# Mirrored output pairs for an inverse DFT: eight matmuls and a flip for two tiles, in place of sixteen matmuls

## The chip, the cores and the metric

The kernel runs on one core of one Trainium2 chip. The metric is the device time of a whole run in microseconds (us). The kernel before takes about 265.7 us. Engines as the profile names them: PE is TensorE (PEld its weight loads), DVE is VectorE, ACT is ScalarE, POOL is GpSimd, SP issues most DMAs. An eviction is ScalarE's copy of a TensorE result out of the accumulators. The granted clock is the share of its full clock that TensorE's throttle let through.

## The reference, cut to what matters

Two branches over x = A_q (2048 x 640) are mixed by a gate. Branch A is a long convolution along the sequence; branch B is an MLP mixer.

```python
x = A_q
g = sigmoid((x * gate_w).sum(-1, keepdims=True))
# A: a 4-tap shift of k, times v; long convolution with ssm_k by FFT; skip ssm_D; times q
y = irfft(rfft(pad(kv)) * rfft(pad(ssm_k)))[:S];  a = x * (y + kv * ssm_D)
# B: h = gelu(layernorm(x) @ w1); shifted groups @ w2; x1 = x + .;  b = x1 + gelu(layernorm(x1) @ w3) @ w4
return g * a + (1 - g) * b
```

## The kernel before

The convolution is done by matmuls with DFT matrices. The sequence is four blocks (b) of 512; a forward DFT of k*v and one of the filter give spectra in four parts (j). VectorE multiplies them in eight "units": for each half of the 640 columns (hh = 0, 1) the four parts j. `final` then transforms back, multiplies by q, adds branch B and stores. Each of the 16 output tiles of a half needs all four products of its half, so the second half's inverse starts when the last unit is nearly done.

```python
def inverse(hh, t, o_gy):                 # one tile: 8 matmuls of 320 columns, 1 eviction with the gate
    c, q = t // 4, t % 4
    o = ps(1, "inv")[:, 0:320]
    pairs = [(G[:, j, r, 128*q:128*(q+1)], slots[order.index((j, hh))][:, r, c, :]) for j in range(4) for r in range(2)]
    mm(o, pairs)
    act(o_gy, o, ACTF.Copy, scale=gst[3][:, t:t+1])

def final(hh, t0, k):                     # two tiles
    qt, gy = qb[k % 3], gyb[k % 6]
    P.dma(sp, qt, A_q[...])
    for i in range(2): inverse(hh, t0 + i, gy[:, i, :])
    tt(gy, gy, qt, ALU.mult)              # VectorE, 640 columns
    tt(gy, gy, X[:, t0:t0+2, hs], ALU.add)
    P.dma(sp, out[...], gy)

# ... main part: layer norm 1, mm1, gate, filter (h_load, h_fold, h_chunk), mm2, layer norm 2, k*v and x_fwd,
#     units 0-3, mm3/mm4, units 4-7, then final for both halves
sched = P.schedule({"warm": 1, ..., "inv": 3})    # static list scheduling, with a table of tuned priorities
```

Every instruction is recorded, and a list scheduler with its own assumed durations and a table of tuned priorities (`BIASES`) fixes the order on each engine. An experiment that leaves the record alone and only changes what is emitted therefore keeps the order of all queues ("in the same order").

Of the kernel before, what the change touches and what calls it, by code (L numbers as in the profile page):

```python
# [455 lines left out]
def _folded_dft():  # L456


    n = np.arange(256, dtype=np.float64)[:, None]
    k = np.arange(256)[None, :]  # L460
    w = 2 * np.pi / 1024
    R = np.stack([np.cos(w * 2 * k * (n + .5)),
                  -np.sin(w * np.where(k == 0, 512, 2 * k) * (n + .5)),
                  np.cos(w * (2 * k + 1) * (n + .5)),
                  -np.sin(w * (2 * k + 1) * (n + .5))])
    m = np.arange(512, dtype=np.float64)[None, :] + 1
    k = np.arange(256)[:, None]
    G = np.stack([np.where(k == 0, 1., 2.) * np.cos(w * 2 * k * m),
                  np.where(k == 0, -np.cos(np.pi * m), -2. * np.sin(w * 2 * k * m)),
                  2. * np.cos(w * (2 * k + 1) * m),  # L470
                  -2. * np.sin(w * (2 * k + 1) * m)]) / 1024
    R = R.reshape(4, 128, 2, 256).transpose(1, 0, 2, 3)
    G = G.reshape(2, 2, 2, 128, 512).transpose(3, 0, 2, 1, 4)
    return R.reshape(128, 4 * 2 * 256), G.reshape(128, 8 * 512)


def bass_gated_mix__ssm_conv_h3__mixer_s_mlp__prompt_kernel(
# [6 lines left out]
    Rm, Gm = _folded_dft()  # L484
# [28 lines left out]
    def ps(n, cls):  # L513
# [3 lines left out]
    BIASES = {'combine-0-1|dve': 112800.0,  # L517
     'combine-0-2|dve': 390500.0,
     'combine-0-3|dve': 148700.0,
     'combine-1-1|dve': -1084300.0,  # L520
     'combine-1-2|dve': 347400.0,
     'combine-1-3|dve': 360330.0,
     'const-G|sp': -800400.0,
     'const-R|pool': -1708200.0,
     'const-d|act': 438800.0,
     'const-esel|act': 542800.0,
     'const-gelu|act': 628600.0,
     'const-gsum|act': 714800.0,
     'const-gsum|pe': -693600.0,
     'const-gw|act': 134300.0,  # L530
     'const-id|act': 597700.0,
     'const-set|dve': -259200.0,
     'const-shk|sp': -476510.0,
     'const-taps|act': 71300.0,
     'const-taps|pe': -1183000.0,
     'const-w10|act': 411500.0,
     'const-w11|act': 99500.0,
     'const-w12|act': -82200.0,
     'const-w13|act': 542600.0,
     'const-w14|act': -177900.0,  # L540
     'const-w2|sp': -1367890.0,
     'const-warm|dve': -419000.0,
     'const-warm|pe': -1163200.0,
     'final-0-0-0|act': -51500.0,
     'final-0-0-0|dve': -1092800.0,
     'final-0-0-0|pe': 687900.0,
     'final-0-0-0|sp': -820700.0,
     'final-0-10-5|act': -15410.0,
     'final-0-10-5|dve': -1158800.0,
     'final-0-10-5|pe': 557340.0,  # L550
     'final-0-10-5|sp': 461170.0,
     'final-0-12-6|act': -92500.0,
     'final-0-12-6|dve': -1109900.0,
     'final-0-12-6|pe': 401300.0,
     'final-0-12-6|sp': 456500.0,
     'final-0-14-7|act': 28600.0,
     'final-0-14-7|dve': -1185300.0,
     'final-0-14-7|pe': -1521100.0,
     'final-0-14-7|sp': 323940.0,
     'final-0-2-1|act': -83700.0,  # L560
     'final-0-2-1|dve': -1058900.0,
     'final-0-2-1|pe': 738600.0,
     'final-0-2-1|sp': -843000.0,
     'final-0-4-2|act': -10700.0,
     'final-0-4-2|dve': -1213400.0,
     'final-0-4-2|pe': 766400.0,
     'final-0-4-2|sp': -769300.0,
     'final-0-6-3|act': -43700.0,
     'final-0-6-3|dve': -1162570.0,
     'final-0-6-3|pe': 711200.0,  # L570
     'final-0-6-3|sp': 481500.0,
     'final-0-8-4|act': -39900.0,
     'final-0-8-4|dve': -1064120.0,
     'final-0-8-4|pe': 800700.0,
     'final-0-8-4|sp': 461110.0,
     'final-1-0-8|act': -51700.0,
     'final-1-0-8|dve': -1101500.0,
     'final-1-0-8|pe': -1292900.0,
     'final-1-0-8|sp': 324000.0,
     'final-1-10-13|act': 29400.0,  # L580
     'final-1-10-13|dve': -1294800.0,
     'final-1-10-13|pe': -1198700.0,
     'final-1-10-13|sp': 453900.0,
     'final-1-12-14|act': -58400.0,
     'final-1-12-14|dve': -1216300.0,
     'final-1-12-14|pe': -1210000.0,
     'final-1-12-14|sp': 453840.0,
     'final-1-14-15|act': 20000.0,
     'final-1-14-15|dve': -1322800.0,
     'final-1-14-15|pe': -1210100.0,  # L590
     'final-1-14-15|sp': 478240.0,
     'final-1-2-9|act': -32500.0,
     'final-1-2-9|dve': -1136100.0,
     'final-1-2-9|pe': -1207100.0,
     'final-1-2-9|sp': 398170.0,
     'final-1-4-10|act': -28730.0,
     'final-1-4-10|dve': -1148500.0,
     'final-1-4-10|pe': -1188100.0,
     'final-1-4-10|sp': 416500.0,
     'final-1-6-11|act': 6000.0,  # L600
     'final-1-6-11|dve': -1298570.0,
     'final-1-6-11|pe': -1216900.0,
     'final-1-6-11|sp': 402000.0,
     'final-1-8-12|act': -24100.0,
     'final-1-8-12|dve': -1307870.0,
     'final-1-8-12|pe': -1216900.0,
     'final-1-8-12|sp': 399100.0,
     'gate|act': -995000.0,
     'gate|pool': -1672500.0,
     'h_chunk-0|act': 397020.0,  # L610
     'h_chunk-0|pe': -699300.0,
     'h_chunk-1|act': 450090.0,
     'h_chunk-1|pe': -697690.0,
     'h_chunk-2|act': 508000.0,
     'h_chunk-2|pe': -625500.0,
     'h_chunk-3|act': -993600.0,
     'h_chunk-3|pe': -1160800.0,
     'h_chunk-4|act': -1010000.0,
     'h_chunk-4|pe': -1435500.0,
     'h_fold-0|act': 145500.0,  # L620
     'h_fold-0|dve': -284700.0,
     'h_fold-0|pe': -1207100.0,
     'h_fold-1|act': -37700.0,
     'h_fold-1|dve': -197300.0,
     'h_fold-1|pe': -1201040.0,
     'h_fold-2|act': 392940.0,
     'h_fold-2|dve': -120000.0,
     'h_fold-2|pe': -1054820.0,
     'h_fold-3|act': -1149200.0,
     'h_fold-3|dve': -555600.0,  # L630
     'h_fold-3|pe': -1213500.0,
     'h_fold-4|act': -1124600.0,
     'h_fold-4|dve': -306510.0,
     'h_fold-4|pe': -1277300.0,
     'h_load-0|sp': -960300.0,
     'h_load-1|sp': -969600.0,
     'h_load-2|sp': -1606660.0,
     'h_load-3|sp': -1633300.0,
     'h_load-4|sp': -1079370.0,
     'kv_block-0-0|act': -1000100.0,  # L640
     'kv_block-0-0|dve': 314100.0,
     'kv_block-0-0|pe': -1476900.0,
     'kv_block-0-0|sp': -1152780.0,
     'kv_block-0-1|act': -996400.0,
     'kv_block-0-1|dve': -165000.0,
     'kv_block-0-1|pe': -1319800.0,
     'kv_block-0-1|sp': -1599600.0,
     'kv_block-0-2|act': -1175100.0,
     'kv_block-0-2|dve': -164200.0,
     'kv_block-0-2|pe': -1272300.0,  # L650
     'kv_block-0-2|sp': -1734900.0,
     'kv_block-0-3|act': 384900.0,
     'kv_block-0-3|dve': -539400.0,
     'kv_block-0-3|pe': -1091000.0,
     'kv_block-0-3|sp': -1438000.0,
     'kv_block-1-0|act': -856400.0,
     'kv_block-1-0|dve': 329400.0,
     'kv_block-1-0|pe': -1615420.0,
     'kv_block-1-0|sp': -809900.0,
     'kv_block-1-1|act': -883100.0,  # L660
     'kv_block-1-1|dve': 377200.0,
     'kv_block-1-1|pe': -1583170.0,
     'kv_block-1-1|sp': -812500.0,
     'kv_block-1-2|act': -914980.0,
     'kv_block-1-2|dve': 136160.0,
     'kv_block-1-2|pe': -1589800.0,
     'kv_block-1-2|sp': -736200.0,
     'kv_block-1-3|act': -1029040.0,
     'kv_block-1-3|dve': 129530.0,
     'kv_block-1-3|pe': -1426770.0,  # L670
     'kv_block-1-3|sp': -893100.0,
     'ln1-0-1|act': 101830.0,
     'ln1-0-1|dve': -257500.0,
     'ln1-0-1|pe': -755060.0,
     'ln1-0-1|pool': -1698790.0,
     'ln1-1-2|act': 375500.0,
     'ln1-1-2|dve': -257500.0,
     'ln1-1-2|pe': -757290.0,
     'ln1-1-2|pool': -1700830.0,
     'ln1-10-12|dve': -418240.0,  # L680
     'ln1-10-12|pool': -1846860.0,
     'ln1-10-12|sp': -1625900.0,
     'ln1-12-14|dve': -418300.0,
     'ln1-12-14|pool': -1846800.0,
     'ln1-12-14|sp': -1110200.0,
     'ln1-14-16|dve': -511600.0,
     'ln1-14-16|pool': -1715400.0,
     'ln1-14-16|sp': -1670900.0,
     'ln1-2-4|act': 542230.0,
     'ln1-2-4|dve': -435850.0,  # L690
     'ln1-2-4|pe': -1222940.0,
     'ln1-2-4|pool': -1698140.0,
     'ln1-4-6|dve': -260150.0,
# [621 lines left out]
    def final(hh, t0, k):  # L1315
# [3 lines left out]
        for i in range(2):  # L1319
            inverse(hh, t0 + i, gy[:, i, :])  # L1320
# [94 lines left out]
```

## Time and profile before

| | kernel before |
|---|---|
| median of the first three runs | 266.12 us (265.34 to 266.37) |
| profile | span 1490.2 us, PE busy 99% |
| second profile of the same kernel, taken after the prediction | span 263.6 us |

The profile is of an execution unlike the timed ones. These are its first lines and its costliest group (the name, the shape and count, busy us, mean ns of one, idle before):

```profile
span 1490.2 us, 4348 instructions
PE 1468.0 (99%) x1627; PEld 505.4 (34%) x1644; DVE 230.2 (15%) x406; ACT 163.9 (11%) x272; POOL 36.4 (2%) x93
...
L977 PE MATMUL PSall<-arena 128*128 128x320 bf16 x1008 | 842.7, 1210 | 0.0
```

Only TensorE is slow there: VectorE's 230.2 us and ScalarE's 163.9 us would fit a run of 266 us, TensorE's 1468 us would not. So counts, order and the other engines' durations can be used, and waits and chains can't.

I had the unchanged kernel run again (the run b_again below); this is the profile that everything after the prediction is compared with. From its page: busy time, busy tenths in 40 slices of 6.6 us with the granted clock, and the chain of waits that ended last.

```profile
span 263.6 us, 4348 instructions
PE 251.1 (95%) x1627; PEld 154.0 (58%) x1644; DVE 227.2 (86%) x406; ACT 156.8 (59%) x272; POOL 61.5 (23%) x93
...
PE   6799999999999999998999999799999999999993
...
DVE  3664898799999999999999999999999999995442
...
PEclk9779999999999999999999999999999999999999
...
PE 65%; DVE 22%; ACT 4%; POOL 3%; ACTq 2%; issue 2%; DVEq 0%
```

TensorE is at 9 almost everywhere, up to the last slice. VectorE is loosely busy in the first 40 us, then full, and in the last four slices half idle. The chain, two thirds PE, says that TensorE finishes the kernel.

Next, busy time by stretch. I cut at 40 us and at 234.8 us, the end of the last 960-column operation of the last unit ("the marker" below; what follows it is the tail); columns are the stretch, its length, then busy us (and instructions) of PE, PEld, DVE, ACT and POOL, granted clock, DMA.

```profile
0.00:40.00 40.00, 35.72 (x227) 19.65 (x231) 25.62 (x78) 27.63 (x40) 11.83 (x26) 0.91 1.02 258
40.00:234.80 194.80, 190.55 (x1221) 116.79 (x1234) 188.00 (x300) 118.28 (x214) 49.72 (x68) 1.00 0.39 97
234.80:263.60 28.80, 24.78 (x183) 17.61 (x180) 13.62 (x31) 10.83 (x19) 0.00 (x0) 0.98 0.34 92
```

VectorE is idle 14.4 us in the first 40 us, 6.8 us in the next 195, and 15.2 us at the end.

### The profile page before, as it was taken

Reading aid. Unit: us, or ns where it says so; the run is one execution under the profiler, and the core shown is the slowest. Engines: PE = TensorE matmul, PEld = TensorE weight load, DVE = VectorE, ACT = ScalarE, POOL = GpSimd, SP = SyncE. Lnnn points to the kernel's source line nnn. Section 1 sums busy time; section 2 is a strip of 40 time slices with the busy share of each in tenths; the row PEclk is TensorE's granted clock in tenths of the full one; section 3 lists DMA queues with packets and bytes.
Section 4 is the critical chain, followed back from the end, with each engine's and each line's share of the span. In section 5 each row is a group of like instructions: output and inputs, shape, how many; then the busy total and the mean of one; then the engine's idle time right before and its main releaser. Section 6 shows DMA issues by size and latency. Waiting matters only on the chain.

```text
span 1490.2 us, 4348 instructions
## 1 busy us (share of the span) xinstructions
PE 1468.0 (99%) x1627; PEld 505.4 (34%) x1644; DVE 230.2 (15%) x406; ACT 163.9 (11%) x272; POOL 36.4 (2%) x93
## 2 busy tenths in 40 slices
PE   9999999999999999999999999999999999999998
PEld 2333333233333333232332233333233332333343
DVE  2013002112022102214061000031030213000000
ACT  1111112111111111111001000000000000000000
POOL 1000100000000000000000000000000000000000
DMA  5112012000021100200000000000000000000010
GB/s 155 27 50 71 1 43 53 24 15 25 11 57 36 24 4 1 75 26 11 0 9 0 0 0 0 0 13 26 0 9 0 9 5 0 4 5 0 22 27 13
DMA packets 55865, 31.79 MB, mean 21 GB/s; under 512 B 27432, under 2 KB 54308, under 8 KB 55716
## 3 DMA queue, kind: packets, MB, share of 16 engines
q1 hardware_dynamic: 48988, 30.06, 7.5%
q10 hardware_dynamic: 6712, 0.92, 0.4%
q0 software_dynamic: 144, 0.52, 0.1%
q8 instruction: 13, 0.21, 0.1%
q14 instruction: 8, 0.07, 0.0%
HBM read 24.29 MB, written 2.62 MB: 18 GB/s over the span
## 4 chain that ended last, share of the span: by engine, by line
PE 99%; issue 1%; ACT 0%; DVE 0%
PE PSall L977 96%; PE PSall L1001 2%; PE PSall L1180 0%; ACT arena L969 0%; PE PSall L1032 0%; DVE arena L959 0%; DVE arena L997 0%; DVE arena L988 0%; DVE arena L987 0%; DVE arena L990 0%; DVE arena L994 0%; DVE arena L993 0%; DVE arena L992 0%; DVE arena L989 0%; DVE arena L991 0%
## 5 line engine op out<-in xcount | busy, mean ns | idle before, releaser
L977 PE MATMUL PSall<-arena 128*128 128x320 bf16 (+4 forms) x1584 | 1437.8, 1274 | 15.9 <-issue 10.3
L977 PEld LDWEIGHTS PSall<-arena 128*128 128x128 bf16 (+1 forms) x1601 | 496.1, 316 | 959.3 <-issue 955.1
L959 DVE TENSOR_TENSOR arena<-arena 128x640 bf16<-128x640 bf16 (+6 forms) x289 | 195.2, 716 | 882.9 <-ACT arena L969 862.7
L969 ACT ACTIVATE arena<-PSall 128x512 bf16<-128x512 f32 (+4 forms) x168 | 115.7, 701 | 759.3 <-PE PSall L977 725.4
L969 ACT ACTIVATE arena<-PSall,arena 128x320 bf16<-128x320 f32 (+1 forms) x48 | 29.6, 616 | 561.2 <-PE PSall L977 561.2
L964 DVE TENSOR_SCALAR arena<-arena 128x640 bf16<-128x640 bf16 (+3 forms) x52 | 20.2, 394 | 294.9 <-POOL arena L1139 138.6
L964 POOL TENSOR_SCALAR arena<-arena 128x1 f32<-128x1 f32 (+2 forms) x60 | 17.3, 293 | 874.4 <-ACT arena L969 760.6
L1001 PE MATMUL PSall<-arena 128*128 128x512 bf16 x18 | 24.6, 1663 | 2.3 <-DVE arena L997 2.3
L969 ACT ACTIVATE arena<-arena 128x640 bf16<-128x640 bf16 (+3 forms) x23 | 17.2, 754 | 0.0
L1139 POOL TENSOR_TENSOR arena<-arena 128x1 f32<-128x1 f32 (+1 forms) x25 | 16.9, 675 | 1.9
L1135 DVE BATCH_NORM_STATS2 arena<-arena 128x6 f32<-128x320 bf16 x32 | 14.0, 476 | 4.5 <-DMA arena<-in_A_q_dram 4.4
L964 DVE TENSOR_SCALAR arena<-PSall 128x4 f32<-128x4 f32 x4 | 0.6, 162 | 73.7 <-PE PSall L977 73.7
L1001 PEld LDWEIGHTS PSall<-arena 128*128 128x128 bf16 x18 | 3.8, 235 | 13.9 <-issue 11.5
L1180 PE MATMUL PSall<-arena 128*128 128x128 bf16 x20 | 7.3, 666 | 0.0
L1180 PEld LDWEIGHTS PSall<-arena 128*128 128x128 bf16 x20 | 4.8, 283 | 3.1 <-issue 1.7
L969 ACT ACTIVATION_READ_ACCUMULATOR arena<-PSall 128x1 f32 x16 | 3.1, 195 | 0.0
L969 ACT ACTIVATION_READ_ACCUMULATOR arena<-arena 128x1 f32 x16 | 3.1, 194 | 0.0
L1136 DVE BATCH_NORM_AGGREGATE arena<-arena 128x2 f32<-128x12 f32 x16 | 3.0, 196 | 0.1
L1032 PEld LDWEIGHTS PSall<-arena 128*4 128x4 bf16 x5 | 0.8, 202 | 2.7 <-DMA arena<-in_A_ssm_k_dram 2.7
L959 POOL TENSOR_TENSOR arena<-arena 128x16 f32<-128x16 f32 x3 | 1.3, 449 | 13.9 <-DVE arena L964 13.8
L1032 PE MATMUL PSall<-arena 128*4 128x128 bf16 x5 | 1.6, 633 | 0.0
L969 ACT ACT_TABLE_LOAD x1 | 1.3, 1283 | 2.3 <-issue 2.3
(16 smaller groups left out, 4.5 us busy)
## 6 DMA issues: line engine op xcount, KB each, us to landing
arena<-in_A_k_dram SPq DMA_DIRECT2D x14, 400.0 KB, 3.8
arena<-in_A_q_dram SPq DMA_DIRECT2D x20, 160.0 KB, 2.5
arena<-in_A_ssm_k_dram SPq DMA_DIRECT2D x5, 512.0 KB, 4.8
arena<-in_A_v_dram SPq DMA_DIRECT2D x16, 160.0 KB, 2.7
out_dram<-arena SPq DMA_DIRECT2D x16, 160.0 KB, 1.9
arena<-in_A_q_dram SPq DMA_DIRECT2D x3, 640.0 KB, 5.8
arena<-in_B_w_dram SPq DMA_DIRECT2D x1, 1920.0 KB, 8.4
arena<-in_B_w_dram SPq DMA_DIRECT2D x1, 1152.0 KB
```

The costliest lines, as they stand in the source:

```text
L959: P.op(eng, lambda e: e.tensor_tensor(o, a, b, op), [a, b], [o], dve_ns(o, [a, b], 2) if eng == "dve" else 500)
L964: P.op(eng, lambda e: e.tensor_scalar(o, real(a), s1, s2, op0=op0, **({} if op1 is None else {"op1": op1})), [a] + aps, [o], dve_ns(o, [a] ...
L969: P.op("act", lambda e: e.activation(o, real(a), f, bias=bias, scale=scale, **({"accum_out": accum} if accum is not None else {})), [a] + ...
L977: fns.append(lambda e, l=l, r=r, i=i: e.matmul(real(o), l, r, start=(i == 0), stop=(i == len(pairs) - 1)))
L1001: P.op("pe", [lambda e: e.matmul(real(pw), warm[:, 0:128], warm[:, 128:640], start=True, stop=True)] * 2, [warm], [pw], 856.0)
L1032: P.op("pe", [lambda e, c=c: e.transpose(real(psb)[:, 128 * c:128 * (c + 1)], shk_sb[:, 4 * c:4 * c + 4], ident) for c in range(DC)], [shk ...
L1135: P.op("dve", lambda e, o=o, i=i: e.bn_stats(o, i), [i], [o], 400)
L1136: P.op("dve", lambda e: e.bn_aggr(bna[:, t, :], bns[k]), [bns[k]], [bna[:, t, :]], 120)
L1139: P.op("pool", lambda g: g.tensor_tensor(o, a, e, ALU.pow), [a, e], [o], 450 + 400 * n_of(o))
L1180: P.op("pe", [lambda e, c=c, pb=pb, xn=xn: e.transpose(real(pb)[:, 128 * c:128 * (c + 1)], xn[:, 128 * c:128 * (c + 1)], ident) for c in r ...
```

## The change

Sample the output at half offsets (m + 1/2) instead of m + 1. Then tile q and tile 3 - q of a block are mirror images: half of the terms are even, half odd. Four matmuls give the even sum, four the odd sum; tile q is their sum, tile 3 - q their difference with its rows reversed, and one matmul with a flip matrix reverses them. That is 9 matmuls for two tiles instead of 16. To move the output by half a sample, the filter is transformed at whole offsets, with a matrix of its own: 20 more matmuls of 512 columns (two per chunk with one row of weights for the sample at zero, two per chunk with 32 columns). All priorities were retuned.

```diff
-    def final(hh, t0, k):                # and inverse()
+    def final(hh, c, q, k):              # tiles 4c+q and 4c+3-q
+        P.dma(sp, qt, rows(A_q))
+        ts(qt[:, 0], qt[:, 0], gst[3][:, ts_:ts_ + 1], None, ALU.mult)      # gate, VectorE, 320 columns
+        pr = ps(2, "inv")[:, :, 0:320]
+        for e in range(2):                                                  # even and odd sum
+            mm(pr[:, e], [(G[:, j, e ^ (j // 2), 128 * q:128 * (q + 1)],
+                           slots[order.index((j, hh))][:, e ^ (j // 2), c, :]) for j in range(4)])
+        act(ab, pr, ACTF.Copy)
+        tt(gy[:, 0], ab[:, 0], ab[:, 1], ALU.add)                           # VectorE, 320 columns
+        tt(ab[:, 1], ab[:, 0], ab[:, 1], ALU.subtract)                      # VectorE, 320 columns
+        pf = ps(1, "fl")[:, 0:320]
+        mm(pf, [(flip, ab[:, 1])])
+        act(gy[:, 1], pf, ACTF.Copy, scale=gst[3][:, td:td + 1])
         tt(gy, gy, qt, ALU.mult)
         ...
 def h_chunk(c):                          # filter DFT
-    mm(pr[:, r, :], [(Rt[...], ev[:, eo, kk, :]) for kk in range(2)])
+    pairs = [(Rh[...], ev[:, eo, kk, :]) for kk in range(2)]
+    if y == 0:
+        pairs.append((ones[0:1, :], ev[0:1, 1, 0, :]))
+    mm(pr[:, r, :], pairs, low=[(Zn[:, kk, :], ev[:, 0, kk, :]) for kk in range(2)] if j == 0 and r == 1 else [])
 ... (new tables, a second filter matrix loaded, buffers moved, all of BIASES replaced)
```

## The prediction

> **What bounds the kernel now.** The profile is not of an execution like the timed ones: its span is 1490.2 us, the timed runs took 265.34 to 266.37 us (median 266.12). In it TensorE is busy 99% and 320-column matmuls start 843 ns apart. That can't be the pace of the timed runs: the recorded matmul shapes add up to 564k columns, which in 266 us need at least 2.12 columns per ns. So I use the profile for counts, order and the durations of the other engines, not for its idle times or its chain of waits ("PE 99%").
>
> The Trainium skill ("TensorE: Matmul & The Clock Gate", Back-to-back issue gap) gives N/2.4+2.5 ns for a warm matmul; this trace shows no such pace. As an estimate it makes 136 ns of a 320-column matmul and 239 us of all 1627: 90% of 266. VectorE is busy 230.2 us (the page's first part), 87% of 266; ScalarE 163.9. So TensorE and VectorE bound it together.
>
> The timeline's order shows the end: after VectorE's last unit come four mm4 tiles as filler, then all 16 inverse tiles of the second half: 128 matmuls, about 17.4 us, beside 16 VectorE operations of 0.49 us. That tail is TensorE-bound, about 21 us with the last eviction (0.53), two VectorE operations and the store (1.9).
>
> **Removed.** The inverse goes from 256 matmuls of 320 columns to 128 and 16 flips: -112, -15 us of TensorE, half in the tail.
>
> **Added.** TensorE: in the filter DFT 20 more 512-column matmuls, +4.3 us; h_fold has 40 more matmuls but the same columns. VectorE: per pair a gate multiply, an add and a subtract of 320 columns. Such operations take 318 ns in the trace, 235 start to start; with about 0.2 us for the multiply 0.67 us per pair, +11 us in all: half among the second half's units, half in the tail. ScalarE: 16 x (704+527) for 32 x 527 ns, +3 us, off the path. DMA: 0.54 MB more at the start.
>
> **On the critical path.** Tail, per pair: TensorE 9 x 136 ns = 1.2 us (was 2.2), ScalarE 1.2, VectorE about 1.5. So it becomes VectorE-bound: 2 us to fill, 8 x 1.5, 1 us for the last flip, 2 us to store, 17 us for 21: -4 us. Before the tail TensorE loses 3 us net but VectorE gains 5.4. There both had about 17 us of slack (VectorE 222 us of work between 5.7 us and the tail). If VectorE is the tighter, the body grows by up to 5 us and eats the gain; if TensorE, it shrinks by 3. All priorities were retuned too, which may win back slack. I expect a small gain: 263.5 us, 257 to 271. Chances: faster 0.33, same 0.52, slower 0.15.
>
> **What would show it.** Matmuls 1627 to about 1575; VectorE busy up by 10 to 14 us to about 242. In the tail VectorE is dense and matmuls have gaps; in the body VectorE idles less. If VectorE busy rises by 11 us and the time falls over 5, VectorE had slack that the retuned order filled; if the time rises, the body was VectorE-bound.
>
> **What would make it wrong.** If the pace of matmuls is below the estimate, TensorE alone binds and the saving is nearer 10 us. If the flip's round trip (ScalarE, VectorE, TensorE, ScalarE, VectorE) stalls the queues, or three input buffers are too few, the tail doesn't shrink. The new order could be worse, and the later freeing of space for w3 and the MLP could delay those.

## More of the kernel before

In the timeline the end is a steady beat: VectorE does two operations of 640 columns, 1.02 us, every 2.17 us, and waits for an eviction that waits for TensorE.

```profile
249.31 1.02 DVE L959 TENSOR_TENSOR arena<-arena 128x640 bf16<-128x640 bf16 x2 [1.15 <-ACT arena L969]
251.48 1.02 DVE L959 TENSOR_TENSOR arena<-arena 128x640 bf16<-128x640 bf16 x2 [1.15 <-ACT arena L969]
...
216.83 42.75 PE L977 MATMUL PSall<-arena 128*128 128x320 bf16 x286
```

Sixteen matmuls of 320 columns start 136 ns apart (median of this trace), 2.18 us: that is the beat. The last line is TensorE without a gap to 259.6 us.

## The result

| | before | after |
|---|---|---|
| median, fast runs | 265.73 us (4) | 268.34 us (4) |
| ratio | | 1.0103, 95% interval 1.0074 to 1.0131 |
| profiled span | 263.6 us | 267.0 us |

A ratio here and below is the mean time of one kernel's fast runs over that of the kernel before's of the same rounds, so it is not quite the ratio of the quoted medians. The change made the kernel 1.0% slower; I had expected 1.0% faster. The page of the kernel after, the same lines:

```profile
span 267.0 us, 4304 instructions
PE 246.2 (92%) x1592; PEld 144.4 (54%) x1592; DVE 238.1 (89%) x456; ACT 158.1 (59%) x272; POOL 65.0 (24%) x93
...
PE   7499899999999999899999969997999979999880
...
DVE  1354789999999999997999999999999998999996
...
PEclk9979999999999999999999999999999989999996
...
DVE 53%; PE 27%; POOL 8%; DMA 5%; ACT 3%; issue 2%; ACTq 0%; DVEq 0%; POOLq 0%
```

TensorE has more small holes and nothing to do in the last slice. VectorE now works to the end, with 10.9 us more in all (227.2 to 238.1). The chain has turned over: from 65% PE to 53% DVE. By stretch, cut at 40 us and at the end of the same operation of the last unit, now at 245.1 us:

```profile
0.00:40.00 40.00, 33.84 (x236) 17.50 (x236) 21.15 (x71) 26.29 (x35) 7.44 (x19) 0.96 0.88 244
40.00:245.10 205.10, 198.35 (x1261) 117.63 (x1261) 198.24 (x334) 122.18 (x221) 57.59 (x74) 0.99 0.38 92
245.10:267.00 21.90, 14.03 (x99) 9.23 (x96) 18.70 (x54) 9.65 (x17) 0.00 (x0) 0.90 0.51 142
```

The last stretch is 6.9 us shorter (28.8 to 21.9), as intended. The middle is 10.3 us longer (194.8 to 205.1), and VectorE's work in it is 10.2 us longer (188.0 to 198.2), so its idle time there stayed at 6.8 to 6.9 us. Of the 10.2 us, 4.5 us is work that VectorE had done in the first 40 us before (25.6 against 21.2 us), and the other 5.8 us is new. The sum, 10.3 - 6.9 = 3.4 us, is the difference of the spans.

One part of this is not work. The 8 in the PEclk line is a stretch of 3.4 us from 218.1 us on in which TensorE got half its clock; it had waited for VectorE just before (0.7 and 1.2 us). VectorE then waits 1.1 us for an eviction. The profile of the kernel before has no such stretch between 17 and 262 us, and those of a_dve_light and a_filter_light (below) have none between 17 and 258 us. First two lines: the kernel after, the second VectorE's wait; third line: a_filter_light.

```profile
220.00:240.00 20.00, 20.00 (x117) 11.60 (x116) 18.65 (x35) 10.10 (x17) 0.00 (x0) 0.96 0.11 33
223.94 0.69 DVE L977 TENSOR_TENSOR arena<-arena 128x320 bf16<-128x320 bf16 x2 [1.09 <-ACT arena L987]
```

```profile
220.00:240.00 20.00, 20.00 (x129) 12.45 (x128) 19.68 (x39) 9.77 (x17) 0.00 (x0) 1.00 0.03 10
```

So about 1.1 us of the kernel after's 267.0 goes with the clock in this run. Its other three fast runs have mean clocks of 0.971 to 0.980 (0.979 here), but no kept trace; whether the change brings the stretch about was not tested. At the end VectorE hardly waits, and TensorE does:

```profile
257.74 2.47 DVE L977 TENSOR_TENSOR arena<-arena 128x640 bf16<-128x640 bf16 x7
260.13 0.29 DVE L982 TENSOR_SCALAR arena<-arena 128x320 bf16<-128x320 bf16 x1
260.35 1.65 DVE L977 TENSOR_TENSOR arena<-arena 128x640 bf16<-128x640 bf16 x4
...
259.47 0.45 PE L998 MATMUL PSall<-arena 128*128 128x320 bf16 x2 [0.55 <-DVE arena L977]
262.50 0.45 PE L998 MATMUL PSall<-arena 128*128 128x320 bf16 x1 [2.58 <-DVE arena L977]
```

These numbers say where the time went, not why: a busy share can't tell whether VectorE's work was on the path. The theories that I set out with:

- Theory V: the body was VectorE-bound all along, so the added VectorE work was paid for in full.
- Theory F: the filter's 20 matmuls are on the path in the first part.
- Theory O: the retuned order is simply a worse one.

### The profile page after: what moved, and what is told of

Its sections match the earlier page's. It is cut to its first block, busy times and chain, and to the rows that moved or that the text cites. A ratio compares the mean times of both kernels' runs of the same rounds, so it can differ in the third digit from the quotient of the medians.

```text
span 267.0 us, 4304 instructions
## 1 busy us (share of the span) xinstructions
PE 246.2 (92%) x1592; PEld 144.4 (54%) x1592; DVE 238.1 (89%) x456; ACT 158.1 (59%) x272; POOL 65.0 (24%) x93
## 4 chain that ended last, share of the span: by engine, by line
DVE 53%; PE 27%; POOL 8%; DMA 5%; ACT 3%; issue 2%; ACTq 0%; DVEq 0%; POOLq 0%
DVE arena L977 49%; PE PSall L998 27%; POOL arena L982 6%; DVE arena L982 4%; DMA arena<-in_B_w_dram 4%; ACT arena L987 3%; POOL arena L1171 1%; DMA arena<-in_A_k_dram 1%; POOL arena L977 1%; DVE arena L1291 0%; PE PSall L1212 0%; ACTq L229 0%; DVEq L437 0%; POOLq L435 0%
## 5 line engine op out<-in xcount | busy, mean ns | idle before, releaser
L998 PE MATMUL PSall<-arena 128*128 128x320 bf16 (+6 forms) x1549 | 238.4, 313 | 15.2 <-DVE arena L977 8.2
L977 DVE TENSOR_TENSOR arena<-arena 128x640 bf16<-128x640 bf16 (+6 forms) x321 | 201.7, 675 | 13.4 <-DMA arena<-in_A_ssm_D_dram 8.7
L998 PEld LDWEIGHTS PSall<-arena 128*128 128x128 bf16 (+2 forms) x1549 | 140.9, 99 | 112.0 <-issue 14.0
L987 ACT ACTIVATE arena<-PSall 128x640 bf16<-128x640 f32 (+4 forms) x184 | 121.0, 704 | 44.1 <-PE PSall L998 39.6
L982 POOL TENSOR_SCALAR arena<-arena 128x1 f32<-128x1 f32 (+2 forms) x60 | 41.0, 686 | 98.5 <-ACT arena L987 65.3
L987 ACT ACTIVATE arena<-PSall,arena 128x640 bf16<-128x640 f32 (+1 forms) x32 | 20.5, 661 | 43.8 <-PE PSall L998 43.8
L982 DVE TENSOR_SCALAR arena<-arena 128x640 bf16<-128x640 bf16 (+3 forms) x68 | 24.8, 373 | 10.2 <-PE PSall L1212 6.5
L1024 PE MATMUL PSall<-arena 128*128 128x512 bf16 x18 | 6.4, 514 | 1.6 <-DVE arena L1020 1.6
L1024 PEld LDWEIGHTS PSall<-arena 128*128 128x128 bf16 x18 | 1.9, 121 | 4.7 <-issue 2.6
L1212 PE MATMUL PSall<-arena 128*128 128x128 bf16 x20 | 1.8, 220 | 0.0
L1212 PEld LDWEIGHTS PSall<-arena 128*128 128x128 bf16 x20 | 1.2, 98 | 0.7 <-issue 0.5
```

What stands on the lines that cost most here:

```text
L977: P.op(eng, lambda e: e.tensor_tensor(o, a, b, op), [a, b], [o], dve_ns(o, [a, b], 2) if eng == "dve" else 500)
L982: P.op(eng, lambda e: e.tensor_scalar(o, real(a), s1, s2, op0=op0, **({} if op1 is None else {"op1": op1})), [a] + aps, [o], dve_ns(o, [a] ...
L987: P.op("act", lambda e: e.activation(o, real(a), f, bias=bias, scale=scale, **({"accum_out": accum} if accum is not None else {})), [a] + ...
L998: fns.append(lambda e, part=part, l=l, r=r, i=i: e.matmul(real(o)[0:32] if part else real(o), l, r, start=(i == 0), stop=(i == last)))
L1024: P.op("pe", [lambda e: e.matmul(real(pw), warm[:, 0:128], warm[:, 128:640], start=True, stop=True)] * 2, [warm], [pw], 856.0)
L1212: P.op("pe", [lambda e, c=c, pb=pb, xn=xn: e.transpose(real(pb)[:, 128 * c:128 * (c + 1)], xn[:, 128 * c:128 * (c + 1)], ident) for c in r ...
```

## The experiments

Most change the amount of work of one kind in one kernel and keep the order, so what the order is worth stays out of them. Several compute a wrong result. The comparison with the reference can't be leaned on for these: it passed b_pe_light and a_pe_light, which leave out half of the inverse, a_filter_light and the two head experiments, and it failed a_dve_light alone.

**b_again.** The kernel before, unchanged. 

> The kernel before, unchanged, for a profile in the state of the timed runs. All theories: 265 to 266.5 us, TensorE no longer 99% busy, VectorE busy about 228 to 232 us (238.1 in the kernel after). Theory V (the body is VectorE-bound) expects VectorE to be 90% busy or more in most slices between 20 us and the tail, and a tail of about 20 us in which VectorE is below half busy. Theory O (the retuned order is the loss) expects the stretch up to 130 us to be shorter than in the kernel after. Theory F (the filter's added matmuls are on the path) expects the TensorE-dense stretch before 80 us to end about 4 us earlier than in the kernel after.

Measured: 265.72 us (ratio 1.0017, 0.9980 to 1.0055); its profile is shown above. VectorE is busy as V expected, but the tail is 28.8 us and not about 20, and the chain is 65% PE, which V did not expect.

**a_dve_light.** The kernel after, the three added VectorE operations cut to 16 columns.

```diff
-        tt(gy[:, 0], ab[:, 0], ab[:, 1], ALU.add)
+        P.op("dve", lambda e: e.tensor_tensor(gy[:, 0, 0:16], ab[:, 0, 0:16], ab[:, 1, 0:16], ALU.add),
+             [ab[:, 0], ab[:, 1]], [gy[:, 0]], d)      # recorded as before; the multiply and the subtract alike
```

> The kernel after in the same order, but the gate multiply, the add and the subtract that were added per pair are emitted with 16 columns instead of 320 (a wrong result on purpose). About 0.45 us less VectorE work per pair, 7 us in all. Theory V: 5 to 7 us less, 261 to 263.5 us. Theory O or F alone: under 2 us less, 266.5 to 268.5 us.

Measured: 263.76 us (ratio 0.9938, 0.9907 to 0.9968), so 4.6 us less than the kernel after (just short of what V expected), for 5.2 us less VectorE busy time (238.1 to 232.9). The marker comes at 240.1 us instead of 245.1, and the tail is 21.6 us instead of 21.9. The 5.0 us before the tail are 3.6 us less VectorE work (219.4 to 215.8), 1.0 us less idle time between 40 us and the marker, where this run lacks the half-clock stretch, and 0.4 us at the start. So before the tail VectorE's added work is on the path in full; in the tail, 1.5 us less of it gained only 0.3 us.

**b_pe_light.** The kernel before, half of the inverse's matmuls not emitted: the change's saving on TensorE (and a little more) without its cost.

```diff
-        mm(o, pairs)
+        use = pairs[0::2]      # 4 of 8, recorded as 8
```

> The kernel before in the same order, with 4 of the 8 matmuls of each inverse tile left out (a wrong result on purpose): 128 matmuls less, 17 us of TensorE by my estimate, 8.7 us of it in the tail. My prediction's tail (TensorE-bound) expects 6 to 9 us less from the tail alone, 257 to 260 us, and if TensorE also bounds the body, up to 15 us less. Rival: the tail is already bound by eviction, VectorE or output, then under 3 us less.

Measured: 259.08 us (ratio 0.9766, 0.9733 to 0.9799), about 6 us less, for 128 matmuls less, which at 136 ns are 17.4 us. So TensorE did bind the kernel before, but only for some 6 us; then something else takes over, and the chain says what. Where the 6 us come from is seen by laying the two traces side by side, instruction by instruction (VectorE's are the same, in the same order): up to 237 us VectorE's start no earlier than in b_again (0.8 us later, as they do at 10 us already), and all is gained in the tail, 21.6 for 28.8 us. The half of the saving that falls into the first half's inverse gained nothing before it.

```profile
PE 236.8 (92%) x1499; PEld 141.3 (55%) x1516; DVE 226.9 (88%) x406; ACT 155.4 (60%) x272; POOL 63.0 (24%) x93
...
DVE 51%; PE 29%; DMA 8%; ACT 4%; issue 3%; POOL 3%; ACTq 1%; DVEq 0%
```

**b_dve_heavy.** The mirror of a_dve_light: the kernel before with the added VectorE work of the first half's 8 pairs, and no saving.

```diff
+        f = [V(oKV + 4096 + 960 * (k % 3) + 320 * i, 320) for i in range(3)]        # only if hh == 0; dead space
+        fill = [tensor_scalar(f[0], qt[:, 0], 1.0), tensor_tensor(f[1], qt[:, 0], qt[:, 1], ADD), tensor_tensor(f[2], .., SUBTRACT)]
-        tt(gy, gy, qt, ALU.mult)
+        P.op("dve", fill + [multiply], ...)                                         # recorded as the multiply alone
```

> The kernel before in the same order, with the three 320-column VectorE operations that the change adds (one multiply, one add, one subtract) put in front of the multiply of each of the 8 pairs of the first half, into space that is no longer used; the result stays right. In the kernel after the step of a 320-column add or subtract is 281 ns and of the multiply 229 ns (starts to starts), 0.79 us per pair, 6.3 us in all; these here don't wait for each other, so 0.7 us, 5.6 us. Theory V (the body is VectorE-bound): 4.5 to 6.5 us over the kernel before, 269.5 to 272 us, all of it before the tail, which stays at about 23.5 us. If VectorE had slack in the body: under 2 us more.

Measured: 266.05 us (ratio 1.0009, 0.9981 to 1.0037): no cost. VectorE was busy 4.8 us more (232.0), and the last unit's marker moved from 234.8 to 239.7 us, but the tail shrank from 28.8 to 24.3 us, because TensorE's queue went on as before.

```profile
PE 251.1 (95%) x1644; PEld 153.6 (58%) x1644; DVE 232.0 (88%) x430; ACT 156.6 (59%) x272; POOL 63.5 (24%) x93
...
PE 65%; DVE 22%; ACT 4%; ACTq 3%; POOL 3%; issue 1%; DVEq 0%
```

Theory V falls: the body did become longer by the added work, but the kernel did not. The kernel before was TensorE-bound in what ended last, and VectorE, 97% busy as it was between 40 and 234.8 us, had 5 us to spare.

**a_filter_light.** The kernel after without the 20 added matmuls of the filter (`pairs[:2]` emitted, `low` dropped). 

> The kernel after in the same order without the 20 added 512-column matmuls of the filter DFT (a wrong result on purpose). Theory F: 3 to 4.5 us less, 264 to 265.5 us. Theories V and O: within 1.5 us of the kernel after (268.3).

Measured: 264.76 us (ratio 0.9981, 0.9955 to 1.0007), 3.6 us less than the kernel after, as Theory F expected. The first k*v product starts 3.0 us earlier (31.7 for 34.7 us) and so does what follows, up to 218 us; VectorE's busy time in the first 40 us rises from 21.2 to 24.0 us. Its wait for TensorE's transposes, the longest of which was 5.5 us in the kernel after (first line: the waits of VectorE in the kernel after; second: in a_filter_light; total us, times, longest us), gets shorter:

```profile
DVE arena L982 <- PE PSall L1212: 6.5, 2, 5.5
```

```profile
DVE arena L982 <- PE PSall L1215: 4.3, 2, 3.2
```

The two traces side by side say what the 20 matmuls cost. Eight of them run between 19.8 and 28 us, eight between 40 and 52 us, four between 70 and 73 us. Only the first eight matter for VectorE: 0.7 us of the 3.0 was there before the first of them, 2.3 us come at this one wait, and from there to 218 us the distance stays at 2.6 to 3.0 us. Another 1.2 us, at 224 us, is the half-clock stretch that this run lacks. The lines below are the filter's matmuls just before the transposes that VectorE waits for (the kernel after, then a_filter_light):

```profile
20.44 6.97 PE L998 MATMUL PSall<-arena 128*128 128x512 bf16 x27
```

```profile
19.36 4.67 PE L1103 MATMUL PSall<-arena 128*128 128x512 bf16 x20
```

Seven more matmuls take 2.3 us more, 330 ns each and not 216. In the trace of the kernel after the next matmul starts 317 ns after one with a single row of weights and 269 ns (mean) after one with 32 columns, and the full one before them takes 309 to 319 ns in place of 216. By these steps all 20 take about 7 us of TensorE, where I had predicted 4.3.

**b_filter_heavy.** The mirror: the kernel before with 20 of its own filter matmuls done twice (the first of a group, with start set, so the second overwrites it). 

> The kernel before in the same order, with 20 of the filter DFT's 512-column matmuls done twice, two or one in each group, so many and as long as the change adds (4.3 us of TensorE by estimate); the result stays right. Theory F (the first 90 us are TensorE-bound): 2.5 to 4.5 us more, 268 to 270 us. If it is the place that the filter's matmuls have in the new order, ahead of the layer norm's transposes, that costs, and not their number: under 1.5 us more.

Measured: 270.02 us (ratio 1.0153, 1.0114 to 1.0192), 4.4 us more: as much as 20 x 216 ns. So in the old order their number costs, without the place that the new order gives them. Here it adds up over a longer time: against b_again VectorE's instructions are 1.2 us late at 33 us, 3.0 at 50 us and 4.9 at 106 us. In the new order only the eight early ones delay VectorE, so there the place counts too. Nor is this quite the mirror that I meant: its repeats are full matmuls of 216 ns, shorter than those of the change.

**a_old_prio.** The changed structure with the old priorities. 

> The changed structure with the priorities of the kernel before (the pairs' carried over by number). Theory O (the retuned order is the loss) expects at most 268 us, no worse than the kernel after. Theories V and F expect nothing of it by themselves; if priorities fit one structure only, it is well over 270 us.

Measured: 277.37 us, one run, of unknown state. So far as one run tells, a table of priorities fits one structure; this tells nothing more.

After these I replaced V by **theory X**: the kernel before was TensorE-bound with VectorE about 5 us behind. The change takes some 11 us from TensorE (112 x 136 - 20 x 216 ns; with the 7 us above for the second term, about 8) and gives VectorE 11 us, and so makes it VectorE-bound.

**a_pe_light.** The kernel after, with half of the inverse matmuls (64) not emitted, as in b_pe_light. 

> The kernel after in the same order, with 4 of the 8 inverse matmuls of each pair left out (a wrong result on purpose): 64 matmuls less, about 8.7 us of TensorE. In the kernel before, leaving out 128 gave 6.2 us. Theory X (the change has made a TensorE-bound kernel into a VectorE-bound one): under 1.5 us less, about 267 to 268.5 us. If TensorE still bounds the end of the kernel: 3 to 6 us less.

Measured: 269.89 us (ratio 1.0150, 1.0126 to 1.0175): no gain from 8.7 us (64 x 136 ns) less of TensorE; about 1.5 us slower, rather. Theory X holds up to the tail: side by side with the kernel after, VectorE's instructions are 0.5 us early at 35 us and still 0.5 us early at 251 us, so the 32 matmuls left out of the first half gained nothing. The chain is the same as with all matmuls:

```profile
PE 239.2 (89%) x1510; PEld 137.8 (51%) x1528; DVE 238.1 (89%) x456; ACT 157.6 (59%) x272; POOL 65.0 (24%) x93
...
DVE 53%; PE 28%; POOL 6%; DMA 5%; ACT 4%; issue 2%; ACTq 0%; DVEq 0%
```

Why it is slower isn't settled; it is in the tail alone (23.5 for 21.9 us). In the stretch from 250 to 260 us the granted clock is 0.83, where the kernel after has 1.00, and TensorE waits there more; that fits, and wasn't tested.

**a_retuned and b_retuned.** Theory O needed its own test: the priorities of both structures searched anew in the same way (random changes, kept by the makespan of the kernel's own scheduler, with two of its assumed durations corrected by the traces; its figures say nothing about the chip). 

> The structure of the kernel after, its priorities searched anew with the kernel's own scheduler, after I had corrected two of its assumed durations by the traces (35 ns more for each VectorE operation, 5 us more for the two loads of single elements). Theory O (the order is what loses): 264 us or less, so that the change itself would be a gain. Theory X: the structure moves work from one bound engine to the other, so 265 to 269 us.

 

> The same search for the structure of the kernel before, for a fair comparison with a_retuned. The kernel before has been tuned long: 262 to 268 us. What tells is the difference to a_retuned: under 2 us either way says that the two structures are worth the same once both are tuned alike; over 4 us in favour of a_retuned says that theory O is right.

Measured: a_retuned 268.59 us (ratio of its fast runs 1.0071, 1.0032 to 1.0110; one of its four runs was slow, 274.76 us, and is left out of the ratio), b_retuned 264.02 us (0.9931, 0.9889 to 0.9973). The two are 4.6 us apart, in favour of the old structure. So the changed structure did not get below the old kernel with a second order either, and the old structure gained 0.7%. That speaks against O. It is one search for each, though, and a_retuned's chain is 68% PE: with VectorE at 237.2 us and TensorE at 243.2 us of busy time, its order makes them wait for each other in other places. That no better order of the changed structure exists is not shown.

**r_m_tuned and all_r_tuned.** If VectorE is what the change overloads, the pair should be put together elsewhere. TensorE can do it: the even and odd sums, evicted once, go through an identity and an identity for the one tile, a flip and a negative flip for the other, and the gate goes back into the evictions. That is 12 matmuls per pair (16 before, 9 in the change), no added VectorE work, and two evictions of 320 columns beside the one of 640.

```diff
+        for i, (t, l0, l1) in enumerate(((ts_, ident, ident), (td, flip, nflip))):
+            pf = ps(1, "fl")[:, 0:320]
+            mm(pf, [(l0, ab[:, 0]), (l1, ab[:, 1])])
+            act(gy[:, i], pf, ACTF.Copy, scale=gst[3][:, t:t + 1])
-        tt(gy[:, 0], ab[:, 0], ab[:, 1], ALU.add)
-        tt(ab[:, 1], ab[:, 0], ab[:, 1], ALU.subtract)      # and the flip, and the gate multiply
```

r_m_tuned does this in the first half only, where VectorE has the units to do, and keeps the change's form in the tail, where VectorE has room; all_r_tuned does it everywhere. The priorities were searched as above, for somewhat longer. 

> A third version: in the first half the pair is recombined by TensorE (identity and flip matmuls on the evicted sums, the gate in the evictions, nothing more on VectorE), in the second half as in the kernel after; priorities searched in the same way. Against the kernel after it has 6.3 us less VectorE work and 3.3 us more of TensorE (24 matmuls of 320 columns), and about 4 us more of ScalarE. Theory X: it beats the kernel after by 3 to 7 us, 261 to 265 us. If the order is all that counts: no better than a_retuned.

 

> As r_m_tuned, but all 16 pairs are recombined by TensorE: VectorE has nothing more to do than in the kernel before (busy about 227 us), TensorE 64 matmuls of 320 columns less and 20 of 512 more than the kernel before, ScalarE about 11 us more; priorities searched in the same way. Theory X expects it near r_m_tuned (262.2 us), 259 to 265 us, and its tail bound by ScalarE (per pair 704 + 2 x 528 ns). If VectorE also binds the tail, it is 2 to 5 us below r_m_tuned.

Measured: r_m_tuned 262.16 us (ratio 0.9835, 0.9782 to 0.9888), all_r_tuned 262.15 us (0.9901, 0.9841 to 0.9961). Both beat the kernel before and the kernel after. r_m_tuned is also about 1% faster than b_retuned of the same chip and rounds (0.9835 against 0.9931). Their profiles have TensorE and VectorE both below their old peaks of the two kernels (r_m_tuned):

```profile
PE 245.4 (95%) x1600; PEld 146.4 (56%) x1616; DVE 231.7 (89%) x432; ACT 162.4 (63%) x280; POOL 60.0 (23%) x93
...
DVE 47%; PE 35%; POOL 6%; DMA 6%; issue 2%; ACT 2%; SPq 0%
```

The chain is now mixed. all_r_tuned has VectorE at 226.3 us and a chain of 73% PE: with VectorE relieved altogether, TensorE binds again, so freeing VectorE in the tail too brought nothing more. My expectation that ScalarE would bind that tail was wrong: ACT has 6% of its chain. The orders differ between these versions, so the 1% is of structure and order together.

**a_no_dwait and a_head_both.** In the first 40 us of the kernel after VectorE waits 8.7 us for the load of ssm_D, which the new order puts ahead of the layer norm's sums. Is that wait part of the 4.5 us that VectorE is behind at 40 us? ssm_D was replaced by a column that lies in memory.

```diff
-        tt(k[:, 0, 0:1], k[:, 0, 0:1], Dcol[:, c:c + 1], ALU.add)
+        ... tensor_tensor(k[:, 0, 0:1], k[:, 0, 0:1], ones[:, c:c + 1], ALU.add), and the dependence on the load dropped
```

> The kernel after (the same order but for one memset), with ssm_D replaced in its one use by a column of ones that lies in memory already, so that VectorE no longer waits for that load (a wrong result on purpose). If the wait at the head is on the path: 2 to 5 us less, 263.5 to 266.5 us, and VectorE busy 23 us or more in the first 40 us. If the head is bound by TensorE and the loads of w1 and x: under 1 us less.

 

> a_no_dwait and a_filter_light together. If both waits are on the path one after the other: the sum of the two, 6 to 8 us less than the kernel after, 260 to 262.5 us. If the ssm_D wait is hidden: as a_filter_light, 264 to 265.5 us.

Measured: a_no_dwait 267.97 us (ratio 1.0099, 1.0057 to 1.0141), as the kernel after, with VectorE busy 21.25 us in the first 40 us for 21.15. The queue then waits at the same place for the load of ssm_k, 5.7 us, so only about 3 us of the wait was taken away; none of that came through (side by side with the kernel after, VectorE's instructions start within 0.3 us of the same times from 35 to 220 us). a_head_both 267.14 us (1.0043, 0.9982 to 1.0103), above what either theory expected. Its runs spread from 264.6 us, with a granted clock of 0.986, to 267.0 to 268.1 us, with 0.972 to 0.978. The profile is of the first: its span is 262.8 us and VectorE's busy time in the first 40 us 23.9 us, the same as a_filter_light (262.9 and 24.0 us). So by the profiles 2.8 of the 4.5 us at the head come back without the filter's added matmuls (0.7 of them by an earlier start), and those 3 us of waiting for ssm_D are hidden. Where the other 1.6 us come from, and what the rest of that wait costs, stays open.

## Why the prediction was wrong, point by point

- *The pace of TensorE.* Right. I took 136 ns per 320-column matmul from the Trainium skill ("TensorE: Matmul & The Clock Gate", Back-to-back issue gap) against the 843 ns of the trace at hand; the trace of a normal run has 136 ns (median, both kernels). That it fits is partly luck: the section calls this formula the isolated gap and gives other figures for a stream (see the end).
- *"TensorE and VectorE bound it together."* Near, and not enough. The order is TensorE first, VectorE some 5 us behind: 4.8 us more of VectorE cost nothing (b_dve_heavy), 17.4 us less of TensorE gave 6 us, all in the tail (b_pe_light). With two engines this close, the effect of a trade depends on which is ahead, and no profile at hand could tell it.
- *The tail.* Right in kind and a little small: I had 17 us for 21, -4 us; the tail is 21.9 us for 28.8, -6.9 us, with TensorE idle at its end. That it became VectorE-bound is not shown: less VectorE work in it gained 0.3 us (a_dve_light), less TensorE work nothing (a_pe_light).
- *VectorE busy up by 10 to 14 us.* Right: 10.9 us. In place it is dearer than I had counted: the steps of the 52 operations of 320 columns average 281 ns, not 235, since many wait for the one before (350 ns then).
- *Matmuls 1575.* It is 1592, because the first trace lacked 17 records (1644 - 112 + 60 = 1592).
- *The step that failed: "Before the tail TensorE loses 3 us net but VectorE gains 5.4. There both had about 17 us of slack", and the small gain drawn from it.* It adds up work without regard to when it falls, and one term of the sum is too small. The added filter matmuls take about 7 us of TensorE, not 4.3, so against the 7.6 us saved in the first half's inverse next to nothing is left of the 3 us net. And the two don't meet. Eight of the 20 fall before 28 us, where VectorE waits for TensorE, and lengthen that wait by 2.3 us; a_filter_light as a whole is 3.6 us faster, about 1 us of it by the clock in the profiled runs. The 7.6 us saved fall mostly after 160 us, where VectorE is full, and can't pay that back: a_pe_light, and b_pe_light in the old kernel, show that less TensorE work there moves no VectorE instruction before the tail. VectorE's new work before the tail is paid for: 3.6 us less of it gained as much (a_dve_light); that all 5.8 us count follows from the sum below. Nor was the slack what I took it for: of VectorE's idle time before the tail, 14.4 us lie in the first 40 us, before its work is ready, and 6.8 us in the 195 us after. The kernel after has 6.9 us there, so its order won none of that back.

The sum as the runs have it, as an estimate: with TensorE out of the way the old kernel ends at 259.1 us (b_pe_light); 5.8 us of new VectorE work before the tail and 3.6 us that VectorE is behind that run at 40 us (21.2 us of work done for 24.7) make 268.5; measured 268.3. The tails of the two are alike, 21.6 and 21.9 us. The 1.1 us of the clock stretch are not in this sum; other idle time was smaller by as much.

## What to carry to other kernels

Before trading work from one engine to another, find out how far the second is behind the first: lighten the one and load the other, in the same order, and read the two times. When two engines are within a few per cent, a trade at par is worth at most that distance and costs the rest. And put each added or saved microsecond where it falls in time: work added at the start, where a second engine waits for it, isn't paid for by work saved later on, while that second engine is full. And an added operation of an unusual shape may cost more than its size says: take its step from a trace.

## What the Trainium skill lacked or had wrong

- "TensorE: Matmul & The Clock Gate", Back-to-back issue gap, gives about 131 ns (N=512) and 81 ns (N=128) as the sustained spacing in a stream of weight loads and matmuls, and calls N/2.4 + 2.5 the isolated gap. Here the stream follows that second formula: 216 ns at 512, 136 ns at 320 and 56 ns at 128 columns (medians, weight loads between all), and no step of 512 columns was under 215 ns.
- The same page knows a clock of one half, of 13/16 with three busy cores, and in a caveat one stuck at a quarter. The first profile had a slower pace than these, 843 ns for 320 columns and 1279 ns for 512, about six times the normal, on one core for all of 1490 us, with a reported clock of 1.000. Nothing in the profile but the times themselves shows it.
- No page gives the cost of a matmul with one row of weights, or 32 columns, put among full ones. Here such matmuls took 317 and 269 ns (mean) to the next start, and the full one before them 309 to 319 ns instead of 216.
- "Trainium Kernel Development and Optimization", Performance Expectations, calls matmul busy time a bad measure of the distance to the roofline. That fits: TensorE's busy share fell from 95% to 92% with 6 us gained (b_pe_light) and from 92% to 89% with nothing gained (a_pe_light). But the share of weight loads, which it recommends, moved alike (58% to 55%, 54% to 51%); only the experiment told them apart.
- "GPSIMD Engine Reference", Specifications, says that GpSimd shares its memory interfaces with VectorE, and gives no size there (other pages do, for other operations). Its 50 operations on one column took 296 ns on average where VectorE was 15% busy (the first profile), 717 ns in the same kernel where it was 86% busy (b_again) and 774 ns where it was 89% busy (the kernel after). That this is the contention was not tested.

```profile
L964 POOL TENSOR_SCALAR arena<-arena 128x1 f32<-128x1 f32 x50 | 14.7, 296 | 744.8 <-ACT arena L969 737.4 <-DVE arena L1136 6.5
```

```profile
L982 POOL TENSOR_SCALAR arena<-arena 128x1 f32<-128x1 f32 x50 | 38.6, 774 | 77.6 <-ACT arena L987 65.3 <-DVE arena L1168 10.3
```
